# Spreading the out-projection matmuls between the score bursts, and letting turned results share the value banks

## The chip, the cores and the metric

The kernel runs on one core of a Trainium2 chip. The metric is device time in microseconds, as the median of several runs. The ratio of two kernels is the mean time of the one's fast runs over the mean time of the other's fast runs from the same rounds, so it is not quite the ratio of the medians that are quoted. All runs here are classed as fast. Yet they have two levels, which the granted TensorE clock tells apart: the kernel before takes 399.7 to 402.0 us (once 403.0) when the mean granted clock is 0.999 or more, and 402.8 to 404.6 us when it is 0.987 to 0.992. So a difference of one per cent is read below from the traces (the length of a batch), not from the medians alone.

Engine names in the profile: PE is TensorE, PEld its weight loads, DVE is VectorE, ACT is ScalarE, POOL is GpSimd.

## The reference

Causal attention with 16 extra keys per head, then a gated feed-forward block:

```python
B, H, S, Nb, D = 8, 8, 576, 16, 64
k_all = concat([beacon_k, k]); v_all = concat([beacon_v, v])
scores = q @ k_all.T / 8             # causal mask on the 576 own keys
a = softmax(scores); attn = a @ v_all
x = attn.transpose(0, 2, 1, 3).reshape(B * S, H * D)        # 4608 x 512
g = x @ w_gate; val = x @ w_val                             # 512 x 1536
out = (gelu(g) * val) @ w_out                               # 1536 x 512
```

## The kernel before

Batch `b` of the attention is interleaved with the out-projection of token chunk `b - 1`, so that TensorE has work while ScalarE makes exponentials. The heads go in pairs `m = 0..3`. A pair has four score chunks; chunks 0 and 2 ("ab") and then 1 and 3 ("cd") go through two PSUM buffers `s`. Chunk 1 has to wait until the exponential of chunk 0 has read its buffer, and chunk 3 likewise for chunk 2. After the attention of a batch, the gate and value matmuls of a chunk run in one stretch of 96 matmuls of 512 columns.

The kernel lays out PSUM as eight banks: four for `s`, two for the values `x`, one for out-projection sums `o`, and one spare bank `t` (which also takes the sum of the first of a chunk's four output rows). A finished out-projection sum is evicted, that is, VectorE copies it out of its bank.

```python
def attend(b, m, wide=False):                   # values: 30 matmuls of 65 columns
    x_ps = psum_x.tile([P, 1024], FP32, name="x_ps", tag="x")   # two banks, one tile
    # (wide: the same from psum_s)
    ...
            c0 = SLOT[j] + hi * DV              # j = 0,1,2 in the first bank, 3,4 in the second
            ... mm(x_ps[:, c0 : c0 + DV], expT[...], v_sb[...]) ...

def normalize(b, m):
    ...
    for c0, j0, n in ((0, 0, 6), (512, 6, 4)):  # first bank, second bank
        reciprocal(r, x[:, :, D:DV])
        tensor_tensor(out=y_sb[:, j0 : j0 + n, :], in0=x[:, :, 0:D], in1=r, op=mult)

def turn(b, m):                                 # transposes of the normalized result
    y_ps = psum_t.tile([P, 1024], BF16, name="y_ps", tag="t")
    for j in (4, 3, 2, 1, 0):
        transpose(y_ps[:, Q_LO[j] : Q_LO[j] + n], y_sb[0:n, j, :])
    tensor_copy(xT_sb[:, m, b * S : (b + 1) * S], y_ps[:, 0:S])
...
# batches 1 to 7; o(n) issues the next n of 48 out matmuls (12 per 128 rows of output)
o(6); ab(0); o(10); cd(0); o(8)
for m in range(1, NPAIR):
    ab(m)
    av(m - 1)                                   # attend + normalize
    cd(m)
    o(6 if m < NPAIR - 1 else 5)
    turn(b, m - 1)
av(3); o(7); turn(b, 3)
```

`keep(...)`, left out here, holds every engine to program order. The waits between engines are not written by hand: the language derives them from the tiles that an instruction reads and writes.

The softmax here doesn't subtract the row's maximum and nothing guards it: scores larger than these inputs give would overflow.

Of the kernel before, what the change touches and what calls it, by code (L numbers as in the profile page):

```python
# [7 lines left out]
P = 128  # L8
B, H, S, NB, D = 8, 8, 576, 16, 64
# [8 lines left out]
NPAIR = H // 2  # L18
# [3 lines left out]
S_LO = [0, 112, 240, 368, 496]  # L22
# [17 lines left out]

Q_LO = [0, 112, 240, 368, 448]
SLOT = [0, 2 * DV, 4 * DV, 512, 512 + 2 * DV]
QK_SCALE = 0.125

FP32 = mybir.dt.float32
BF16 = mybir.dt.bfloat16
# [7 lines left out]
def kernel(  # L54
# [12 lines left out]
    nc = tc.nc  # L67
    keep = tc.keep_in_program_order
# [9 lines left out]
    psum_t = ctx.enter_context(tc.tile_pool(name="psum_t", bufs=1, space=bass.MemoryType.PSUM))  # L78
# [3 lines left out]
    ident = const.tile([P, P], BF16, name="ident", tag="ident")  # L82
# [4 lines left out]
    xT_sb = const.tile([P, NPAIR, N_TOK], BF16, name="xT_sb", tag="xT_sb")  # L87
# [56 lines left out]
    def load_v(b):  # L144
        load_keys(v, beacon_v, v_ring[b % NRING][:, :, :, 0:D], b)
# [9 lines left out]
    def mm(out_ap, lhsT, rhs, start, stop, **kw):  # L155
        keep(nc.tensor.matmul(out_ap, lhsT, rhs, start=start, stop=stop, **kw))  # L156

    def act(out_ap, in_ap, func, **kw):
        keep(nc.scalar.activation(out_ap, in_ap, func, **kw))  # L159
# [27 lines left out]
    def warm(b, m, n):  # L187
        w_ps = psum_o.tile([P, D_MODEL], FP32, name="w_ps", tag="o")
        for _ in range(n):
            mm(w_ps, ident, qkT[:, m, 1, 0:512], True, True)  # L190
# [14 lines left out]
    def scores(b, m, c):  # L205
        i = b * NPAIR + m
        if c == 0:
            exp_of[i] = epool.tile([P, 2, EXP_W], BF16, name="expT", tag="expT")
        expT = exp_of[i]
        s_ps = psum_s.tile([P, 2, 512], FP32, name="s_ps", tag="s")  # L210
        for t, s_lo, w, col in CHUNKS[c]:
            for hi in range(2):
                r = slice(64 * hi, 64 * hi + 64)
                mm(
                    s_ps[:, hi, col : col + w],
                    qkT[r, m, 1, t * P : (t + 1) * P],
                    qkT[r, m, 0, NB + s_lo : NB + s_lo + w],
                    True,
                    True,
                )  # L220
        o, w = CHUNK_OFF[c], CHUNK_W[c]
        act(expT[:, :, o : o + w], s_ps[:, :, 0:w], ACT.Exp, scale=QK_SCALE)
        if b:
            masks(b, m, c)
# [29 lines left out]
    def attend(b, m, wide=False):  # L254
        i = b * NPAIR + m
        if wide:
            x_ps = psum_s.tile([P, 1024], FP32, name="xs_ps", tag="s")
        else:
            x_ps = psum_x.tile([P, 1024], FP32, name="x_ps", tag="x")
        expT, v_sb = exp_of.pop(i), v_ring[b % NRING]  # L260
        x_of[i] = x_ps
        for j in range(5):
            for hi in range(2):
                c0 = SLOT[j] + hi * DV
                for t in range(j + 1):
                    e0 = EXP_OFF[t] + Q_LO[j] - S_LO[t]
                    mm(
                        x_ps[:, c0 : c0 + DV],
                        expT[0 : KROWS[t], hi, e0 : e0 + P],
                        v_sb[0 : KROWS[t], t, 2 * m + hi, 0:DV],  # L270
                        t == 0,
                        t == j,
                        skip_group_check=True,
                    )

    y_of = {}

    def normalize(b, m):
        i = b * NPAIR + m
        x_ps = x_of.pop(i)  # L280
        r_sb = npool.tile([P, 10, 1], FP32, name="r_sb", tag="r_sb")
        y_sb = npool.tile([P, 10, D], BF16, name="y_sb", tag="y_sb")
        y_of[i] = y_sb
        for c0, j0, n in ((0, 0, 6), (512, 6, 4)):
            x = x_ps[:, c0 : c0 + n * DV].rearrange("p (j d) -> p j d", d=DV)
            r = r_sb[:, j0 : j0 + n, :]
            keep(nc.vector.reciprocal(r, x[:, :, D:DV]))  # L287
            keep(
                nc.vector.tensor_tensor(  # L289
                    out=y_sb[:, j0 : j0 + n, :], in0=x[:, :, 0:D], in1=r.to_broadcast([P, n, D]), op=ALU.mult  # L290
                )
            )

    def turn(b, m):
        y_sb = y_of.pop(b * NPAIR + m).rearrange("p (j e) d -> p j (e d)", e=2)
        y_ps = psum_t.tile([P, 1024], BF16, name="y_ps", tag="t")
        for j in (4, 3, 2, 1, 0):
            n = P if j else S_LO[1]
            keep(nc.tensor.transpose(y_ps[:, Q_LO[j] : Q_LO[j] + n], y_sb[0:n, j, :], ident[0:n, 0:n]))  # L299
        keep(nc.vector.tensor_copy(xT_sb[:, m, b * S : (b + 1) * S], y_ps[:, 0:S]))  # L300


    h_of, o_of = {}, {}
# [26 lines left out]
    def out_mms(ci, u0, u1, wide=lambda ti: False):  # L330
        for u in range(u0, u1):
            ti, fi = divmod(u, F_TILES)
            if u == 0:
                o_of[ci] = [opool.tile([P, 4, D_MODEL], FP32, name="o_sb", tag="o_sb"), None]
            if fi == 0:
                if wide(ti):
                    o_of[ci][1] = psum_t.tile([P, D_MODEL], FP32, name="o_ps", tag="t")
                else:
                    o_of[ci][1] = psum_o.tile([P, D_MODEL], FP32, name="o_ps", tag="o")
            o_sb, o_ps = o_of[ci]  # L340
            mm(
                o_ps,
                h_of[ci][:, fi, ti * P : (ti + 1) * P],
                wo_sb[:, fi, :],
                fi == 0,
                fi == F_TILES - 1,
            )
            if fi == F_TILES - 1:
                keep(nc.vector.tensor_copy(o_sb[:, ti, :], o_ps))  # L349
                n0 = ci * CH + ti * P  # L350
                keep(nc.sync.dma_start(out=out[n0 : n0 + P, :], in_=o_sb[:, ti, :]))
# [23 lines left out]
    for b in range(B):  # L375
        u = [0]

        def o(n):
            if b:
                out_mms(b - 1, u[0], u[0] + n, lambda ti: ti == 0)  # L380
                u[0] += n

        def ab(m):
            for c in AB:
                scores(b, m, c)

        def cd(m):
            for c in CD:
                scores(b, m, c)

        def av(m, wide=False):
            attend(b, m, wide)
            normalize(b, m)

        keep(nc.scalar.preload_act_table_set(SET_EXP))
        if b == 0:
            for m in range(NPAIR):
                ab(m)
                if m == NPAIR - 1:
                    for mm_ in (0, 1, 2):  # L400
                        for c in AB + CD:
                            if mm_ == 2 or (mm_ == 1 and c in CD):
                                masks(0, mm_, c)
                    av(0)
                    for c in AB:
                        masks(0, m, c)
                else:
                    transpose_pe(0, m + 1, psum_x, "x")
                    if m == 2:
                        for mm_, cs in ((0, AB + CD), (1, AB)):  # L410
                            for c in cs:
                                masks(0, mm_, c)
                cd(m)
                if 1 <= m < NPAIR - 1:
                    warm(b, m, 5)
            for c in CD:
                masks(0, NPAIR - 1, c)
            av(1)
            av(2, wide=True)
            turn(b, 0)  # L420
            turn(b, 1)
            av(3)
            turn(b, 2)
            turn(b, 3)
        else:
            o(6)
            ab(0)
            o(10)
            cd(0)
            o(8)  # L430
            for m in range(1, NPAIR):
                ab(m)
                av(m - 1)
                cd(m)
                o(6 if m < NPAIR - 1 else 5)
                turn(b, m - 1)
            av(3)
            o(7)
            turn(b, 3)
        keep(nc.scalar.preload_act_table_set(SET_GELU))  # L440
        for fi in range(F_TILES):
            gate_val(b, fi, kk_late=fi == 0)
            if b == 0 and 6 <= fi < 10:
                transpose_pe(1, fi - 6, psum_x, "x")
            if fi == 0:
                if b + 2 < B:
                    load_qk(b + 2)
                    load_v(b + 2)
                if NPERM <= b + 1 < B:
                    transpose_dma(b + 1)  # L450
# [34 lines left out]
```

## Time and profile before

| | before |
|---|---|
| time, median of 4 runs | 400.13 us |
| span of the profiled run | 398.9 us |
| length of a batch (one gate/value start to the next, batches 2 to 7) | 42.45 us |
| of it gate/value, 96 matmuls at 0.216 us | 20.7 us |
| PE waits for exponentials (list of waits) | 11.3 us, 25 times |

The engine shares and the clock row of the page (forty slices of the span, tenths of full clock, 9 is 90% or more):

```profile
PE 368.8 (92%) x2960; PEld 186.1 (47%) x3010; DVE 168.1 (42%) x345; ACT 186.2 (47%) x252; POOL 155.5 (39%) x277
...
PEclk9999999999999999999999999999999999999999
```

PE is the limit, and it has its full clock. The list of PE's waits (engine, line, whom it waited for: us in total, times, longest) shows what the change aims at:

```profile
PE s_ps L156 <- ACT expT L159: 11.3, 25, 0.9
...
PE y_ps L299 <- DVE xT_sb L300: 3.4, 2, 1.9
```

One pair of batch 4 on PE's timeline (start, duration, engine, line, operation, output <- inputs, count; in brackets the idle time before and who ended it):

```profile
190.23 0.59 PE L156 MATMUL s_ps<-qkT 64*128 64x512 bf16 x4
190.75 1.09 PE L156 MATMUL x_ps<-v_sb,expT 128*128 128x65 bf16 x30
191.79 0.38 PE L156 MATMUL s_ps<-qkT 64*128 64x64 bf16 x6
192.63 0.27 PE L156 MATMUL s_ps<-qkT 64*128 64x208 bf16 x2 [0.45 <-ACT expT L159]
192.83 1.47 PE L156 MATMUL o_ps<-wo_sb,hT_sb 128*128 128x512 bf16 x5
194.13 0.44 PE L299 MATMUL y_ps<-ident,y_sb 128*128 128x128 bf16 x5
```

The last score chunk of a pair waits 0.45 us for its buffer, three times in each of seven batches: 9.5 us. The five transposes of a turn stand together; from their start at 194.13 to the next pair at 194.50 they take 0.37 us. Some matmul records are missing from this trace (2960 of 3010), so a group's count can be one short.

VectorE's side of the same pair: the first reciprocal starts at 191.87, although the twelve matmuls of the bank that it reads are the first twelve of the thirty that began at 190.75. The last product, which the first transpose needs, ends at 192.79 + 0.42 = 193.21, which is 1.42 us after PE has gone on from the values to the next scores (191.79).

```profile
191.87 0.20 DVE L287 RECIPROCAL r_sb<-x_ps 128x6 f32<-128x6 f32 x1 [0.85 <-PE x_ps L156]
192.10 0.56 DVE L289 TENSOR_TENSOR y_sb<-x_ps,r_sb 128x384 bf16<-128x384 f32 x1
192.58 0.17 DVE L287 RECIPROCAL r_sb<-x_ps 128x4 f32<-128x4 f32 x1
192.79 0.42 DVE L289 TENSOR_TENSOR y_sb<-x_ps,r_sb 128x256 bf16<-128x256 f32 x1
```

### The profile page before, as it was taken

The page shows a single profiled execution, that of the slowest core. Times are in us where ns is not written, and L with a number is a line of the kernel's source. Part 1 is how long each engine was busy: PE and PEld are TensorE (multiplying, and loading weights), DVE is VectorE, ACT ScalarE, POOL GpSimd, SP SyncE. Part 2 cuts the span into 40 slices and gives each one's busy share as a digit, 9 for nine tenths or more (in the row PEclk, how much of TensorE's full clock was granted, in tenths as well). Part 3 has the DMA queues.
Part 4 walks back from the last instruction along what each step waited for, and adds up shares of the span by engine and source line. Part 5 has one row for each costly group of instructions (what it writes and reads, how often), then busy time and mean ns, then how long its engine had stood idle before and what let it go on. Part 6 is the DMA issues. An engine that isn't in the chain of part 4 may idle for free.

```text
span 398.9 us, 7336 instructions
## 1 busy us (share of the span) xinstructions
PE 368.8 (92%) x2960; PEld 186.1 (47%) x3010; DVE 168.1 (42%) x345; ACT 186.2 (47%) x252; POOL 155.5 (39%) x277
## 2 busy tenths in 40 slices
PE   3878999999989998999899999999899989999996
PEld 1454444544454445544554445444544455444442
DVE  1384653533354425433444335343444254333332
ACT  2752247533772377336653575337723673332210
POOL 8722394781358324940487047903300141000000
PEclk9999999999999999999999999999999999999999
DMA  7999997499109961997089913992042010000012
GB/s 89 180 206 204 175 131 93 51 141 159 58 28 148 137 75 49 116 156 87 30 99 139 117 54 49 161 142 60 30 92 54 30 54 26 2 0 28 26 53 105
DMA packets 139153, 36.23 MB, mean 91 GB/s; under 512 B 126832, under 2 KB 134512, under 8 KB 139120
## 3 DMA queue, kind: packets, MB, share of 16 engines
q0 software_dynamic: 103984, 19.14, 63.7%
q1 hardware_dynamic: 35136, 16.62, 20.3%
q8 instruction: 23, 0.38, 0.4%
q14 instruction: 10, 0.08, 0.1%
HBM read 38.27 MB, written 9.44 MB: 120 GB/s over the span
## 4 chain that ended last, share of the span: by engine, by line
PE 81%; ACT 10%; DVE 4%; issue 2%; DMA 1%; POOL 0%; ACTq 0%; POOLq 0%; DVEq 0%
PE gv_ps L156 46%; PE o_ps L156 24%; ACT expT L159 10%; PE s_ps L156 6%; PE y_ps L299 2%; PE x_ps L156 2%; PE t_ps L168 1%; DVE y_sb L289 1%; DVE qkT L179 1%; DMA kb<-in_beacon_k_dram 1%; DVE expT L236 1%; PE w_ps L156 0%; DVE hT_sb L325 0%; ACT ge_sb L159 0%; POOL qk L110 0%
## 5 line engine op out<-in xcount | busy, mean ns | idle before, releaser
L159 ACT ACTIVATE ge_sb<-gv_ps 128x512 bf16<-128x512 f32 x108 | 64.5, 597 | 160.6 <-PE gv_ps L156 160.6
L325 DVE TENSOR_TENSOR hT_sb<-gv_ps,ge_sb 128x512 bf16<-128x512 f32 x108 | 74.7, 692 | 123.4 <-ACT ge_sb L159 123.4
L159 ACT ACTIVATE expT<-s_ps 128x1024 bf16<-128x1024 f32 (+3 forms) x128 | 101.2, 867 | 36.7 <-PE s_ps L156 36.6
L156 PE MATMUL gv_ps<-xT_sb,wv_sb 128*128 128x512 bf16 x430 | 111.9, 379 | 0.1
L156 PE MATMUL gv_ps<-xT_sb,wg_sb 128*128 128x512 bf16 x414 | 109.9, 379 | 1.0
L239 POOL TENSOR_SCALAR_AFFINE_SELECT expT<-expT 128x256 bf16<-128x256 bf16 (+2 forms) x140 | 51.5, 387 | 142.9 <-ACT expT L159 142.9
L156 PE MATMUL o_ps<-wo_sb,hT_sb 128*128 128x512 bf16 x403 | 100.5, 380 | 2.2 <-issue 1.1
L156 PEld LDWEIGHTS <-wv_sb 128*128 128x128 bf16 x432 | 42.2, 98 | 51.0
L156 PEld LDWEIGHTS <-wg_sb 128*128 128x128 bf16 x432 | 41.5, 98 | 48.3
L156 PEld LDWEIGHTS <-hT_sb 128*128 128x128 bf16 x432 | 38.9, 98 | 45.7 <-issue 1.7
L156 PE MATMUL s_ps<-qkT 64*128 64x336 bf16 (+5 forms) x384 | 39.4, 290 | 13.0 <-ACT expT L159 11.3
L349 DVE COPY o_sb<-o_ps 128x512 f32<-128x512 f32 x36 | 24.9, 691 | 46.3 <-PE o_ps L156 43.9
L110 POOL DMA_DIRECT2D v_sb<-in_v_dram x40 | 33.8, 862 | 14.0 <-DMA wv_sb<-in_moe_w_val_dram 3.6
L156 PEld LDWEIGHTS <-expT 128*128 128x128 bf16 (+1 forms) x960 | 31.1, 97 | 9.6 <-POOL expT L239 8.5
L156 PE MATMUL x_ps<-v_sb,expT 128*128 128x65 bf16 x930 | 33.6, 193 | 0.6 <-DVE y_sb L289 0.6
L289 DVE TENSOR_TENSOR y_sb<-x_ps,r_sb 128x384 bf16<-128x384 f32 (+1 forms) x62 | 30.4, 491 | 2.1
L156 PEld LDWEIGHTS <-qkT 64*128 64x128 bf16 x384 | 15.1, 95 | 30.8 <-issue 22.3
L110 POOL DMA_DIRECT2D q_sb<-in_q_dram x30 | 25.3, 855 | 6.1 <-DMA wo_sb<-in_moe_w_out_dram 6.1
L110 POOL DMA_DIRECT2D k_sb<-in_k_dram x30 | 25.4, 891 | 0.0
L300 DVE COPY xT_sb<-y_ps 128x576 bf16<-128x576 bf16 x32 | 14.5, 453 | 19.0 <-PE y_ps L299 19.0
L287 DVE RECIPROCAL r_sb<-x_ps 128x6 f32<-128x6 f32 (+1 forms) x62 | 11.4, 184 | 22.7 <-PE x_ps L156 22.7
L299 PE MATMUL y_ps<-ident,y_sb 128*128 128x128 bf16 (+1 forms) x160 | 14.1, 218 | 3.4 <-DVE xT_sb L300 3.4
(33 smaller groups left out, 91.2 us busy)
## 6 DMA issues: line engine op xcount, KB each, us to landing
out_dram<-o_sb SPq DMA_DIRECT2D x36, 256.0 KB, 2.0
v_sb<-in_v_dram POOLq DMA_DIRECT2D x24, 128.0 KB, 9.6
q_sb<-in_q_dram POOLq DMA_DIRECT2D x24, 128.0 KB, 4.7
k_sb<-in_k_dram POOLq DMA_DIRECT2D x18, 128.0 KB, 7.5
wg_sb<-in_moe_w_gate_dram POOLq DMA_DIRECT2D x3, 512.0 KB, 11.5
wv_sb<-in_moe_w_val_dram POOLq DMA_DIRECT2D x3, 512.0 KB, 13.3
wo_sb<-in_moe_w_out_dram POOLq DMA_DIRECT2D x1, 1536.0 KB, 23.4
v_sb<-in_v_dram POOLq DMA_DIRECT2D x8, 112.0 KB, 8.1
```

Source lines behind the costliest of these rows:

```text
L110: keep(nc.gpsimd.dma_start(out=out_ap, in_=in_ap))
L156: keep(nc.tensor.matmul(out_ap, lhsT, rhs, start=start, stop=stop, **kw))
L159: keep(nc.scalar.activation(out_ap, in_ap, func, **kw))
L168: keep(nc.tensor.transpose(out_ap, in_ap, ident[0:n, 0:n]))
L179: nc.vector.tensor_copy(qkT[:, m, :, NB:SK].rearrange("p w (t r) -> p w t r", r=6), t_ps[:, 0:2, 0:S].rearrange("p w (r t) -> p w t r", r=6),)
L239: nc.gpsimd.affine_select(out=d, in_=d, pattern=[[0, 2], [1, n]], compare_op=ALU.is_ge, fill=0.0, base=NB if t == 0 else 0, channel_multip ...
L287: keep(nc.vector.reciprocal(r, x[:, :, D:DV]))
L289: nc.vector.tensor_tensor(out=y_sb[:, j0 : j0 + n, :], in0=x[:, :, 0:D], in1=r.to_broadcast([P, n, D]), op=ALU.mult)
L299: keep(nc.tensor.transpose(y_ps[:, Q_LO[j] : Q_LO[j] + n], y_sb[0:n, j, :], ident[0:n, 0:n]))
L300: keep(nc.vector.tensor_copy(xT_sb[:, m, b * S : (b + 1) * S], y_ps[:, 0:S]))
L325: nc.vector.tensor_tensor(out=h_of[ci][:, fi, :], in0=gv_ps[:, 1, :], in1=ge_sb, op=ALU.mult)
L349: keep(nc.vector.tensor_copy(o_sb[:, ti, :], o_ps))
```

## The change

The intent: put out matmuls in front of the "cd" scores, so that the exponentials have freed the buffers when these scores come. Out matmuls then cross the boundary between two output rows inside a group, so their sums get a second bank (`t`). The turned results, which used `t`, move into the unused columns of the value banks: a part in the first bank, a part in the second, each copied out on its own.

```diff
+Y_HI, Y_LO = 800, 1600
...
-        y_of[i] = y_sb
+        y_of[i] = (y_sb, x_ps.bitcast(BF16))
...
     def turn(b, m):
-        y_ps = psum_t.tile([P, 1024], BF16, name="y_ps", tag="t")
-        for j in (4, 3, 2, 1, 0):
-            transpose(y_ps[:, Q_LO[j] : Q_LO[j] + n], y_sb[0:n, j, :])
-        tensor_copy(xT_sb[:, m, b * S : (b + 1) * S], y_ps[:, 0:S])
+        y_sb, y_ps = y_of.pop(b * NPAIR + m)
+        for js, base, q0, q1 in (((4, 3), Y_HI, S_LO[3], S), ((2, 1, 0), Y_LO, 0, S_LO[3])):
+            for j in js:
+                transpose(y_ps[:, c0 : c0 + n], y_sb[0:n, j, :])
+            tensor_copy(xT_sb[:, m, b * S + q0 : b * S + q1], y_ps[:, base : base + q1 - q0])
...
-                out_mms(b - 1, u[0], u[0] + n, lambda ti: ti == 0)
+                out_mms(b - 1, u[0], u[0] + n, lambda ti: ti % 2 == 0)
...   # batch 0
-            av(1); av(2, wide=True); turn(b, 0); turn(b, 1); av(3); turn(b, 2); turn(b, 3)
+            av(1, wide=True); turn(b, 0); av(2); turn(b, 1); av(3, wide=True); turn(b, 2); turn(b, 3)
...   # batches 1 to 7
-            o(6); ab(0); o(10); cd(0); o(8)
+            o(6); ab(0); o(7); cd(0); o(6)
             for m in range(1, NPAIR):
                 ab(m)
                 av(m - 1)
+                o(3)
                 cd(m)
-                o(6 if m < NPAIR - 1 else 5)
                 turn(b, m - 1)
+                o(4 if m < NPAIR - 1 else 6)
-            av(3); o(7); turn(b, 3)
+            av(3); o(6); turn(b, 3)
```

(The diff is shortened to one statement per call; statements that stood on lines of their own are joined.)

More of the change, by code (lines that the diff above doesn't have):

```diff
@@ L294, in turn @@
     def turn(b, m):
-        y_sb = y_of.pop(b * NPAIR + m).rearrange("p (j e) d -> p j (e d)", e=2)
-        y_ps = psum_t.tile([P, 1024], BF16, name="y_ps", tag="t")
-        for j in (4, 3, 2, 1, 0):
-            n = P if j else S_LO[1]
-            keep(nc.tensor.transpose(y_ps[:, Q_LO[j] : Q_LO[j] + n], y_sb[0:n, j, :], ident[0:n, 0:n]))
-        keep(nc.vector.tensor_copy(xT_sb[:, m, b * S : (b + 1) * S], y_ps[:, 0:S]))
+        y_sb, y_ps = y_of.pop(b * NPAIR + m)
+        y_sb = y_sb.rearrange("p (j e) d -> p j (e d)", e=2)
+        for js, base, q0, q1 in (((4, 3), Y_HI, S_LO[3], S), ((2, 1, 0), Y_LO, 0, S_LO[3])):
+            for j in js:
+                n = P if j else S_LO[1]
+                c0 = base + Q_LO[j] - q0
+                keep(nc.tensor.transpose(y_ps[:, c0 : c0 + n], y_sb[0:n, j, :], ident[0:n, 0:n]))
+            keep(
+                nc.vector.tensor_copy(
+                    xT_sb[:, m, b * S + q0 : b * S + q1], y_ps[:, base : base + q1 - q0]
+                )
+            )
     h_of, o_of = {}, {}
@@ L417 @@
                 masks(0, NPAIR - 1, c)
-            av(1)
-            av(2, wide=True)
+            av(1, wide=True)
             turn(b, 0)
+            av(2)
             turn(b, 1)
-            av(3)
+            av(3, wide=True)
             turn(b, 2)
@@ L427 @@
             ab(0)
-            o(10)
+            o(7)
             cd(0)
-            o(8)
+            o(6)
             for m in range(1, NPAIR):
@@ L433 @@
                 av(m - 1)
+                o(3)
                 cd(m)
-                o(6 if m < NPAIR - 1 else 5)
                 turn(b, m - 1)
+                o(4 if m < NPAIR - 1 else 6)
             av(3)
-            o(7)
+            o(6)
             turn(b, 3)
```

## The prediction

> **What bounds it.** PE is 92% busy (engine shares) and holds 81% of the chain of waits; TensorE clock 1.0. A batch repeats every 42.45 us (chain: gate/value starts at 120.87, 163.32, 205.77). Gate/value is gapless: 96 matmuls at 0.216 us (timeline). The Trainium skill, "TensorE: Matmul & The Clock Gate", section "Wait — 56ns, not 53.3ns?", has 215.7 ns for N=512; this trace agrees. The change touches the other 21.8 us, whose PE work is 48 out matmuls (10.4 us), scores, values, transposes.
>
> **What waits there.** List of waits: PE for the exponentials, 11.3 us in 25 waits. On the timeline, each of 3 pairs per batch shows 0.45 us before the last score chunk: it needs the exponential that only starts 1.42 us after the pair's first scores. 21 x 0.45 = 9.5 us is what the change can win, 2.4%.
>
> **What changes, m=1..3, costed from the timeline** (time from the pair's first scores): scores 0.52, values 1.05, now out x3 0.65, then the last two score chunks from 2.22 to 2.62; the buffer is free at 2.36 and needed about 2.42, so the 0.45 us wait goes. But the turn now follows at 2.62, and its first transpose needs the whole normalization, which ends 1.42 us after the last value matmul (191.80 to 193.22): 3.0. About 0.43 us wait returns there; before, six out matmuls covered it. Then transposes 0.37, out x4 0.86: 4.28 us, against 4.27, but with 7 out matmuls instead of 6 or 5. Saved about 0.5 us a batch after the prelude; the prelude (6/7/6) gains a wait of about 0.2. Net estimate: -2.3 us over seven batches. Out evictions already did not block.
>
> **What it adds.** The turn becomes two groups in the two banks of the value tile, with a copy between: copies of 208 and 368 columns, about 0.26 and 0.34 us (between 0.156 at 16 and 0.453 at 576), +0.15 us of VectorE per turn, off the path. The danger is the order transposes 4,3 / copy / transposes 2,1,0 on one tile. In this trace a reader of half a two-bank PSUM tile waits for the tile's last matmul: the GELU, reading bank 0, starts after the eighth matmul, not the fourth; the first reciprocal starts after all 30 value matmuls, not after 12. If dependencies go by tile, transposes 2,1,0 wait for the first copy: landing 0.23 + copy 0.26 + two handoffs of 0.03 = about 0.5 us of PE idle per turn. In turns 2 and 3 an out eviction (0.69 us) sits before that copy on VectorE, so 0.9 and up to 1.5. About 2.5 us a batch, 17 us over seven. If by bank, nothing.
>
> Batch 0: values of pair 2 now wait for turn 0's copies: +0.5 to +1.5 us.
>
> **Sum.** By tile (I give it 65%): 400.5 - 2.3 + 17 + 1 = about 416. By bank: about 399. I put 413, range 397 to 420; faster 0.06, same 0.34, slower 0.60.
>
> **What would show it.** Waits: PE scores for exponentials falls from 11.3 to under 3 us; a new wait of PE transposes for normalization (y_sb), about 0.4 us x 21; PE transposes for the copy to xT_sb, 28 waits of 0.5 us or more (by tile) or almost none (by bank). Period 42.1 (by bank) or about 44.6 us. Gate/value stretches unchanged.
>
> **What would make it wrong.** Dependencies by bank or by region; PE records hiding a shorter normalization; the out matmuls waiting for evictions at the new boundaries; score buffers freed later than I read.

## The result

The changed kernel takes 422.32 us (median of 4; 421.7 to 423.3) against 400.13 us: ratio 1.0555, 95% interval 1.0525 to 1.0585. It is slower, as forecast, but 2.3 us beyond the top of the range. Its output is correct.

```profile
PE 380.8 (90%) x3010; PEld 184.6 (44%) x3010; DVE 172.1 (41%) x377; ACT 188.3 (45%) x252; POOL 155.5 (37%) x277
...
PEclk9975999999999999999999999999999999999999
```

New is a dent in the clock, in the third and fourth slices (21 to 42 us, the end of batch 0). The list of PE's waits:

```profile
PE x_ps L302 <- DVE xT_sb L304: 14.9, 30, 1.5
PE x_ps L302 <- DVE y_sb L290: 7.8, 21, 0.4
...
PE s_ps L157 <- ACT expT L160: 1.9, 4, 0.9
PE xs_ps L302 <- DVE xT_sb L304: 1.8, 2, 1.4
```

The waits for exponentials are gone but for 1.9 us. In their place stand 7.8 us of transposes (line 302) waiting for the normalization, and 16.7 us of transposes waiting for a copy out of the same tile. The pair that answers to the one shown above:

```profile
202.46 0.58 PE L157 MATMUL s_ps<-qkT 64*128 64x512 bf16 x4
202.97 1.09 PE L157 MATMUL x_ps<-v_sb,expT 128*128 128x65 bf16 x30
203.90 0.81 PE L157 MATMUL o_ps<-wo_sb,hT_sb 128*128 128x512 bf16 x3
204.64 0.48 PE L157 MATMUL s_ps<-qkT 64*128 64x64 bf16 x8
205.49 0.28 PE L302 MATMUL x_ps<-ident,y_sb 128*128 128x128 bf16 x2 [0.37 <-DVE y_sb L290]
206.13 0.32 PE L302 MATMUL x_ps<-ident,y_sb 128*128 128x128 bf16 x3 [0.36 <-DVE xT_sb L304]
206.30 1.03 PE L157 MATMUL o_ps<-wo_sb,hT_sb 128*128 128x512 bf16 x4
```

The eight score matmuls now run in one piece, as intended. The turn is torn in two: its second group starts 0.64 us after its first, where five transposes in a row took 0.37 us in all. VectorE's row shows the dependency: the copy of the first group starts at 205.81 and ends at 206.08, and the second group of transposes starts at 206.13.

```profile
205.81 0.27 DVE L304 COPY xT_sb<-x_ps 128x208 bf16<-128x208 bf16 x1 [0.38 <-PE x_ps L302]
```

Where the 22.0 us of span (398.9 to 420.9) lie, from the starts of the gate/value stretches:

| stretch | before | after | more |
|---|---|---|---|
| start to first gate/value matmul (batch 0's attention) | 32.27 | 35.89 | 3.62 |
| batch 0's gate/value and batch 1's attention | 46.15 | 50.86 | 4.71 |
| each of the next six batches | 42.45 | 44.68 | 2.23 |
| last gate/value start to the end | 65.8 | 66.0 | 0.2 |

Six times 2.23 is 13.4 us, and one more such amount sits in the second row. The other 2.5 us of that row and the 3.6 us of the first are batch 0's: 6.1 us. A view of stretches of time with each engine's busy time and, after POOL, the granted clock shows why. First the changed kernel, then the kernel before:

```profile
27.00:32.00 5.00, 3.18 (x52) 3.02 (x52) 2.14 (x7) 0.00 (x0) 1.72 (x2) 0.50 1.25 205
...
36.00:41.00 5.00, 5.00 (x16) 1.76 (x14) 1.04 (x2) 0.60 (x1) 2.49 (x3) 0.55 1.28 206
```

```profile
27.00:32.00 5.00, 1.87 (x45) 1.80 (x46) 3.52 (x10) 0.00 (x0) 1.53 (x2) 1.00 1.25 205
36.00:41.00 5.00, 5.00 (x25) 2.27 (x24) 2.08 (x3) 1.61 (x4) 2.21 (x3) 1.00 1.28 206
```

From about 27 us to about 41 us the clock of the changed kernel is halved (the trace's clock record has one stretch of 13.65 us at 0.5, apart from the last 1.4 us of the span). In the same five microseconds from 36 to 41, PE gets 16 matmuls through in place of 25. The Trainium skill, "TensorE: Matmul & The Clock Gate", section "What's actually happening", tells of two states, full and half clock, ruled by how busy PE was in windows of about 3.4 us. The trace agrees with the two states and with the windows: 13.65 us are four windows of 3413 ns, the length that the page gives. How busy PE must be in a window, no run here shows.

PE's waits in this stretch, in the changed kernel and then in the kernel before:

```profile
26.67 0.32 PE L302 MATMUL x_ps<-ident,y_sb 128*128 128x128 bf16 x3 [1.49 <-DVE xT_sb L304]
27.43 1.81 PE L157 MATMUL x_ps<-v_sb,expT 128*128 128x65 bf16 x30 [0.44 <-DVE xT_sb L304]
30.84 0.47 PE L302 MATMUL xs_ps<-ident,y_sb 128*128 128x128 bf16 x3 [1.39 <-DVE xT_sb L304]
34.55 0.46 PE L302 MATMUL x_ps<-ident,y_sb 128*128 128x128 bf16 x3 [1.39 <-DVE xT_sb L304]
```

```profile
28.60 0.45 PE L299 MATMUL y_ps<-ident,y_sb 128*128 128x128 bf16 x5 [1.92 <-DVE xT_sb L300]
31.77 0.44 PE L299 MATMUL y_ps<-ident,y_sb 128*128 128x128 bf16 x5 [1.53 <-DVE xT_sb L300]
```

The changed kernel has more waits here, but none as long as the longest of the kernel before.

### The profile page after: what moved, and what is told of

It is laid out like the page before. It is cut to its first block, busy times and chain, and to the rows that moved or that the text cites. A ratio compares the mean times of both kernels' runs of the same rounds, so it can differ in the third digit from the quotient of the medians.

```text
span 420.9 us, 7417 instructions
## 1 busy us (share of the span) xinstructions
PE 380.8 (90%) x3010; PEld 184.6 (44%) x3010; DVE 172.1 (41%) x377; ACT 188.3 (45%) x252; POOL 155.5 (37%) x277
## 4 chain that ended last, share of the span: by engine, by line
PE 72%; DVE 15%; ACT 7%; DMA 2%; issue 2%; POOL 1%; POOLq 0%
PE gv_ps L157 44%; PE o_ps L157 12%; DVE y_sb L290 7%; PE x_ps L157 7%; ACT expT L160 4%; PE s_ps L157 3%; PE x_ps L302 3%; DVE r_sb L288 2%; DVE o_sb L356 2%; DMA qk<-in_k_dram 2%; DVE xT_sb L304 2%; ACT L402 2%; ACT ge_sb L160 1%; PE w_ps L157 1%; POOL qk L111 1%
## 5 line engine op out<-in xcount | busy, mean ns | idle before, releaser
L160 ACT ACTIVATE expT<-s_ps 128x1024 bf16<-128x1024 f32 (+3 forms) x128 | 103.2, 861 | 38.8 <-PE s_ps L157 34.0
L157 PE MATMUL gv_ps<-xT_sb,wg_sb 128*128 128x512 bf16 x432 | 113.8, 383 | 0.0
L157 PE MATMUL gv_ps<-xT_sb,wv_sb 128*128 128x512 bf16 x432 | 113.1, 381 | 0.0
L157 PE MATMUL o_ps<-wo_sb,hT_sb 128*128 128x512 bf16 x432 | 106.8, 379 | 0.0
L157 PE MATMUL s_ps<-qkT 64*128 64x336 bf16 (+5 forms) x384 | 37.0, 291 | 4.2 <-ACT expT L160 1.9
L111 POOL DMA_DIRECT2D v_sb<-in_v_dram x40 | 34.0, 870 | 16.7 <-DMA wv_sb<-in_moe_w_val_dram 3.7
L302 PE MATMUL x_ps<-ident,y_sb 128*128 128x128 bf16 (+1 forms) x150 | 18.5, 221 | 23.7 <-DVE xT_sb L304 14.9
L157 PEld LDWEIGHTS <-expT 128*128 128x128 bf16 (+1 forms) x960 | 33.1, 100 | 11.8 <-issue 6.8
L290 DVE TENSOR_TENSOR y_sb<-x_ps,r_sb 128x384 bf16<-128x384 f32 (+1 forms) x60 | 29.5, 491 | 2.1
L157 PEld LDWEIGHTS <-qkT 64*128 64x128 bf16 x384 | 13.8, 95 | 32.7 <-issue 27.3
L302 PEld LDWEIGHTS <-y_sb 128*128 128x128 bf16 (+1 forms) x160 | 10.8, 100 | 36.5 <-issue 20.7
```

The lines of the kernel that those rows point to most:

```text
L111: keep(nc.gpsimd.dma_start(out=out_ap, in_=in_ap))
L157: keep(nc.tensor.matmul(out_ap, lhsT, rhs, start=start, stop=stop, **kw))
L160: keep(nc.scalar.activation(out_ap, in_ap, func, **kw))
L290: nc.vector.tensor_tensor(out=y_sb[:, j0 : j0 + n, :], in0=x[:, :, 0:D], in1=r.to_broadcast([P, n, D]), op=ALU.mult)
L302: keep(nc.tensor.transpose(y_ps[:, c0 : c0 + n], y_sb[0:n, j, :], ident[0:n, 0:n]))
```

## The experiments

Theory: the loss in the seven later batches is the copy that stands between the two groups of transposes; the waits follow the declared tile, so writing the second bank waits for a copy that reads only the first. The loss in batch 0 is the same wait plus a halved clock. Rivals: the new places of the out matmuls; slow or conflicting accesses to the value banks; a clock that drops for other reasons. Eleven kernels ran, and all gave correct outputs. "Batch" is the usual (median) spacing of the gate/value starts in batches 2 to 7.

| run | time us | ratio to before | batch us |
|---|---|---|---|
| before | 400.1 | 1 | 42.45 |
| changed | 422.3 | 1.0555 | 44.68 |
| a1 batch 0 as before | 416.2 | 1.0380 | 44.68 |
| a2 only batch 0 changed | 406.0 | 1.0121 | 42.45 |
| a3 copies after all transposes | 399.5 | 0.9968 | 42.33 |
| a4 fillers in batch 0 | 420.6 | 1.0484 | 44.68 |
| b1 new places only | 408.1 | 1.0156 | 43.57 |
| b2 shared banks only | 425.6 | 1.0608 | 45.99 |
| b3 turn in the idle out bank | 393.3 | 0.9786 | 41.41 |
| b4 two one-bank value tiles | 388.4 | 0.9664 | 40.82 |
| c1 a3 with the turn later | 399.6 | 0.9935 | 42.34 |
| c2 b4 retimed | 389.1 | 0.9679 | 41.01 |
| c3 a2 with fillers | 403.3 | 1.0048 | 42.45 |

### a1 and a2: batch 0 apart from the rest

a1 is the changed kernel in which batch 0 keeps its old order and a turn through the spare bank; a2 is the kernel before with the new batch 0.

```diff
 # a1, batch 0
-            av(1, wide=True); turn(b, 0); av(2); turn(b, 1); av(3, wide=True); turn(b, 2); turn(b, 3)
+            av(1); av(2, wide=True); turn_t(b, 0); turn_t(b, 1); av(3); turn_t(b, 2); turn_t(b, 3)
```

> The changed kernel with batch 0 alone put back as before (turns into the spare bank, one copy, old order). Theory (batch 0 cost 3.6 us in its own tail and 2.5 us in its gate/value stage through the halved TensorE clock): 416.2 us, mean clock 1.0, seven later batches still 44.68 us each. Rival (the clock drop and the loss come from the seven batches): about 420 to 422 us, clock still 0.98.

> The kernel before with batch 0 alone as in the change. Theory: 406.3 us, a half-clock stretch of some 10 to 14 us between 27 and 41 us, later batches 42.45 us. Rival (batch 0 costs only what its longer VectorE chain explains, 1 us): 401 to 402 us, clock 1.0.

a1 took 416.18 us, a2 406.04 us. a1's profiled run has clock 1.0; a2's has the same 13.7 us at half clock, and its first gate/value stretch is lengthened like the changed kernel's. So batch 0 costs 422.3 - 416.2 = 6.1 us in the changed kernel, and nearly as much alone (406.0 - 400.4 = 5.6 us in a2's own rounds), so it costs this independently of the other batches. The rivals' numbers (420 to 422, and 401 to 402) are excluded.

### a3: the copies after all transposes

```diff
-        for js, base, q0, q1 in parts:          # transposes of a part, then its copy
-            for j in js: transpose(...)
-            tensor_copy(...)
+        for js, base, q0, q1 in parts:
+            for j in js: transpose(...)
+        for js, base, q0, q1 in parts:
+            tensor_copy(...)
```

> The changed kernel with all five transposes of a turn first and both copies after them; same banks, same places. Theory (the transposes 2,1,0 wait for the first copy only because it stands before them in the program and both touch one tile): the waits of transposes for the copy, 14.9 us, vanish; the waits for the normalization, 7.8 us, stay; 406 to 409 us. Rival (writing into the value banks is itself slow, or the turn waits for the normalization anyway and the two waits overlap): 418 to 422 us.

It took 399.54 us, against 422.3: moving two statements takes away the whole loss, more than was expected (406 to 409 us). A batch falls from 44.68 to 42.33 us, 2.35 us for four turns, 0.59 us per turn. That is more than the 0.43 us of idle per turn that the list of waits shows for batches 1 to 7 (12.0 us over 28 turns in a1), because PE's record counts as busy time in which PE could already have gone on: the first two transposes have a record of 0.28 us in the pair shown, but where nothing holds up the next ones they start 0.12 us after the first (b4, below). Batch 0 recovers as well: its first gate/value matmul starts at 31.58 us, and the clock of the profiled run is 0.998. In PE's waits the copy is gone from the transposes and the normalization stays:

```profile
PE x_ps L303 <- DVE y_sb L290: 8.0, 22, 0.4
...
PE s_ps L157 <- ACT expT L160: 1.9, 4, 0.9
```

### a4 and c3: the clock in batch 0

Both put 13 extra matmuls into the gaps of batch 0's end, a4 into the changed kernel, c3 into a2.

```diff
             turn(b, 0)
+            warm(b, 3, 3)
             av(2)
+            warm(b, 3, 6)
             turn(b, 1)
             av(3, wide=True)
+            warm(b, 3, 4)
```

> The changed kernel with 13 idle-filling matmuls put into the gaps of batch 0's tail, nothing else. Theory (PE idles so long in batch 0's tail that its clock is halved for some 13 us, which stretches two value bursts and the first 12 gate/value matmuls): clock 1.0, about 418.5 us although more work is issued. Rival (the halved clock has another cause, or the fillers cost what they win): clock 0.98 or time 422 us and more.

> a2 (batch 0 alone as in the change) with the 13 fillers of a4. Theory (the halved clock costs 2.5 us and more in batch 0, and the fillers keep it whole): clock 1.0 and 402.5 to 404 us against 406.0 of a2. Rival (the clock drop is not worth its look, as a4's time fell by only 1.7 us): 405 to 407 us with clock 1.0.

a4 came out between its two expectations. Its profiled run has the full clock, and the span falls by 3.6 us (420.9 to 417.3), but the median time only by 1.7 us, to 420.6. In a4's runs the time exceeds the span by 1.9 to 3.4 us where nearly all other runs have 1.7 to 1.8; why is open. c3 was run to settle it, and gave 403.32 us against a2's 406.04 (ratios 1.0048 and 1.0121, on different chips; their intervals, 0.9994 to 1.0101 and 1.0056 to 1.0186, overlap). The mean clock of c3's four runs is 0.992 to 0.999, that of a2's 0.983 to 0.987. The clock of c3's profiled run is 1.0 where a2's was halved; a2 first, then c3:

```profile
36.00:41.00 5.00, 4.78 (x16) 1.85 (x15) 0.69 (x1) 0.60 (x1) 2.42 (x3) 0.63 1.28 206
```

```profile
36.00:41.00 5.00, 5.00 (x25) 2.27 (x24) 2.08 (x3) 1.79 (x3) 2.49 (x3) 1.00 1.28 205
```

In a2 the first gate/value start and the stretch after it are later and longer than in the kernel before by 3.12 + 2.35 = 5.5 us; with fillers by 1.92 + 0.22 = 2.1 us. So of batch 0's loss some 3.3 us are the halved clock, and some 2.1 us are the longer waits themselves. These figures include a small shift from before the programs differ: the last scores of pair 2 came at 19.83 us in the kernel before, at 18.77 in a2 and at 19.33 in c3. Counted from there, a2 loses 6.5 us and c3 2.6 us, which makes the clock's share 3.9 us.

### b1 and b2: each part of the change alone

b1 takes the new places but keeps the turn in the spare bank with one copy (and batch 0 as before). b2 takes the shared banks but keeps the old places (batch 0 as before).

```diff
 # b1: before, with only this
-            o(6); ab(0); o(10); cd(0); o(8)
+            o(6); ab(0); o(7); cd(0); o(6)
-    ab(m); av(m - 1); cd(m); o(6 if m < NPAIR - 1 else 5); turn(b, m - 1)
+    ab(m); av(m - 1); o(3); cd(m); turn(b, m - 1); o(4 if m < NPAIR - 1 else 6)
-            av(3); o(7); turn(b, 3)
+            av(3); o(6); turn(b, 3)
 # b2: a1, with these three hunks reversed
```

> Part 1 alone: the kernel before with the new places of the out matmuls and of the turn, but turns still into the spare bank with one copy, batch 0 untouched. Theory: the 0.45 us waits for exponentials go, about 0.37 us for the normalization comes in their place (21 times), and out matmul 24, now in the middle of a group, waits about 0.9 us for the eviction of its only bank (7 times): 402 to 405 us. Rival (the places alone are the loss): 410 us or more.

> Part 2 alone: turns in the value banks in two groups with a copy between, out matmuls over two banks, but the old places; batch 0 as before. Theory (the copy between the groups is the loss, wherever the turn stands; behind an out eviction it costs about 1 us, else 0.5): 416 to 423 us with no wait for the normalization but still 9 to 10 us of waits for exponentials. Rival (the loss needs the new places): 400 to 403 us.

b1 took 408.1 us, between the two expectations. Its waits are those the theory named, but a batch is 1.1 us longer, not 0.3 to 0.7. a3 shows where this lies: it has the same places, the turn in one piece too, but two out banks, and its batch is 43.57 - 42.33 = 1.24 us shorter. In b1's batch 4 the out matmul that waits for the eviction starts 1.38 us after the start of a group of two, which take 0.43 us: 0.95 us lost. In the third pair the next output row begins right after the turn, 0.59 us after its first transpose instead of 0.29 us, when VectorE has just ended the eviction of the row before (205.09 to 205.77, out matmul at 205.83): another 0.30 us, of which the list of waits shows nothing. PE's waits in b1, then in b2:

```profile
PE y_ps L299 <- DVE y_sb L289: 7.8, 21, 0.4
PE o_ps L156 <- DVE o_sb L349: 5.5, 7, 0.8
...
PE s_ps L156 <- ACT expT L159: 1.8, 3, 0.9
```

```profile
PE x_ps L310 <- DVE xT_sb L312: 16.1, 28, 0.8
PE s_ps L157 <- ACT expT L160: 11.1, 24, 0.9
...
PE x_ps L157 <- DVE xT_sb L312: 3.1, 7, 0.4
```

b1 shows why the change wanted the second out bank (5.5 us of out matmuls waiting for an eviction), and that the places alone give the 0.45 us back: the normalization waits 0.37 us where the exponential waited 0.45 us. b2 took 425.6 us, longer than the whole change, with all the waits for the copy and all the waits for exponentials. So the main loss belongs to the shared tile with a copy in its middle, and the new places do not cause it. The 3.1 us of values waiting for the copies (once a batch) were not expected: a turn late in its pair leaves the value tile occupied when the next values come.

### c1: the turn behind the second out group

```diff
 # a3, with
-                turn(b, m - 1)
                 o(4 if m < NPAIR - 1 else 6)
+                turn(b, m - 1)
```

> a3 (both copies last) with each turn moved behind the second out group, so that the normalization is covered. Theory (sharing the value banks keeps the value tile busy until the turn's copies are done, and with the turn last the next pair's values stand 0.5 us behind it): the waits for the normalization (8 us) go, but the values now wait some 0.35 us for the copies, about 20 times: 397 to 400 us, little better than a3. Rival (the tile is free in time): 391 to 394 us.

It took 399.61 us, as expected. The wait for the normalization is gone, and this one has come:

```profile
PE x_ps L157 <- DVE xT_sb L306: 9.2, 22, 1.7
```

Sharing the value tile has a price of its own, then: the next pair's values stand behind the turn's copies. While the tile is one, the turn is either too early for the normalization (a3, 8.0 us) or too late for the next values (c1, 9.2 us).

### b3 and b4: two ways out

b3 starts from the kernel before. It gives the out sums two banks as in the change, and lets each turn use whichever of these two is not accumulating.

```diff
+            def turn_spare(m):
+                turn(b, m, "o" if (u[0] // F_TILES) % 2 == 0 else "t")
-            o(6); ab(0); o(10); cd(0); o(8)
+            o(6); ab(0); o(9); cd(0); o(5)
-    ab(m); av(m - 1); cd(m); o(6 if m < NPAIR - 1 else 5); turn(b, m - 1)
+    ab(m); av(m - 1); o(3); cd(m); o(4); turn_spare(m - 1)
```

> A version meant to win: each turn goes into whichever of the two out banks is not accumulating, one copy, behind the second out group (out groups 6/9/5, then 3 and 4 per pair, then 7); batch 0 as before. Theory (both waits of 0.45 and 0.37 us go, nothing new comes): 391 to 394 us. Rival (once these waits go the exponentials bound the pairs): 397 to 400 us.

b4 is a1 with the value tile declared as two tiles of one bank each. The banks, the columns and the order of instructions on PE in batches 1 to 7 are the change's; in batch 0, where the key and query transposes use the same banks, one copy becomes two.

```diff
-            x_ps = psum_x.tile([P, 1024], FP32, name="x_ps", tag="x")
+            x_ps = tuple(psum_x.tile([P, 512], FP32, name=f"x{s}_ps", tag=f"x{s}") for s in "ab")
...
-                        x_ps[:, c0 : c0 + DV],
+                        x_ps[bank][:, c0 : c0 + DV],
...
-        for js, base, q0, q1 in (((4, 3), Y_HI, S_LO[3], S), ((2, 1, 0), Y_LO, 0, S_LO[3])):
+        for js, y_ps, base, q0, q1 in (((4, 3), xa, Y_HI, S_LO[3], S), ((2, 1, 0), xb, Y_LO - 1024, 0, S_LO[3])):
```

> The changed kernel, batch 0 order as before, with the two-bank value tile declared as two one-bank tiles; same banks, same instruction order in the seven batches (batch 0's key and query copies split in two). Theory (waits go by declared tile, not by bank or region): the waits for the copy vanish, the first reciprocal starts after 12 of 30 value matmuls so the wait for the normalization vanishes too: 391 to 396 us, batches about 41.2 us. Rival (waits go by bank, or the chip's bank conflicts cause them): no change from a1, 416 us.

b3 took 393.31 us. b4 took 388.44 us: the ratio to before is 0.9664 (0.9603 to 0.9726), and it beats both kernels of this study. One pair of b4 on PE's timeline:

```profile
187.70 0.59 PE L157 MATMUL s_ps<-qkT 64*128 64x512 bf16 x4
188.22 0.54 PE L157 MATMUL xa_ps<-v_sb,expT 128*128 128x65 bf16 x12
188.59 0.71 PE L157 MATMUL xb_ps<-v_sb,expT 128*128 128x65 bf16 x18
189.36 0.59 PE L157 MATMUL o_ps<-wo_sb,hT_sb 128*128 128x512 bf16 x2
189.88 0.48 PE L157 MATMUL s_ps<-qkT 64*128 64x64 bf16 x8
190.30 0.29 PE L320 MATMUL xa_ps<-ident,y_sb 128*128 128x128 bf16 x2
190.42 0.33 PE L320 MATMUL xb_ps<-ident,y_sb 128*128 128x128 bf16 x3
190.59 1.03 PE L157 MATMUL o_ps<-wo_sb,hT_sb 128*128 128x512 bf16 x4
```

No wait is left in this pair. The second group of transposes starts 0.12 us after the first; with one tile it was 0.64. And the first reciprocal of this pair starts at 188.79, 0.57 us after the first value matmul, where it was 191.87 - 190.75 = 1.12 us in the kernel before, so the normalization is ready when the turn comes:

```profile
188.79 0.20 DVE L294 RECIPROCAL r_sb<-xa_ps 128x6 f32<-128x6 f32 x1 [0.73 <-PE xa_ps L157]
190.62 0.27 DVE L322 COPY xT_sb<-xa_ps 128x208 bf16<-128x208 bf16 x1 [0.49 <-PE xa_ps L320]
```

Against a1, which has the same batch 0 but for the split copy, both effects follow from the declaration alone, so both waits were made by the declared tile, and neither by the bank nor by the hardware behind it. That using one bank while VectorE reads another is safe is what the Trainium skill states in "PSUM — Partial Sum Buffer", section "PSUM bank collisions raise a hardware error": the unit to guard is the bank (or a 32-partition quadrant of it). b4 agrees: its output is correct with VectorE copying from the first bank (from 190.62) while PE still transposes into the second (until 190.75 by its record).

### c2: b4 retimed

```diff
-            o(6); ab(0); o(7); cd(0); o(6)
+            o(6); ab(0); o(9); cd(0); o(5)
-                o(4 if m < NPAIR - 1 else 6)
+                o(4)
-            av(3); o(6); turn(b, 3)
+            av(3); o(7); turn(b, 3)
```

> b4 (two one-bank value tiles) with out groups 6/9/5 before the first pair, 3 and 4 in every pair and 7 at the end, in place of 6/7/6, 3 and 4, 3 and 4, 3 and 6, 6. Theory (what is left to win is the 0.25 us wait of the first pair's last scores for their buffer): 386 to 387.5 us. Rival (nothing left): 388.4 us or more, as the values of the last pair may now wait for their masks.

It took 389.12 us with a batch of 41.01 us, so nothing was won. The rival was right: the last pair's values now wait for POOL's masks, 1.7 us in seven waits, which is about 0.25 us per batch.

## Why the prediction was right or wrong

- **Direction and main cause: right.** It named the danger, the order "transposes 4,3 / copy / transposes 2,1,0 on one tile", and read from the trace before (GELU after the eighth matmul, reciprocal after the thirtieth) that a reader of half a tile waits for the whole. b4 shows that this is so, by taking away the shared declaration alone.
- **Size of it: right.** "About 2.5 us a batch, 17 us over seven"; a3 measures 2.35 us a batch, 16.5 us. The batch was forecast at 44.6 us and is 44.68. The terms behind it were less good, and that their sum is so close is partly luck: of the 28 waits forecast at "0.5 us or more", and at 0.9 to 1.5 us where an eviction stands before the copy, those of batch 4 idle 0.36, 0.36, 0.48 and 0.52 us, so the eviction adds only about 0.1 us; each turn loses another 0.16 us that the list of waits doesn't show.
- **Waits for exponentials "under 3 us": right**, 1.9 us. **A new wait for the normalization of "about 0.4 us x 21": right**, 7.8 us in 21 waits.
- **"Net estimate: -2.3 us over seven batches": too favourable.** Without the copy's wait (a3) a batch is 42.33 us against 42.45, so 0.8 us over seven. The places alone had hardly a gain to give, since the wait for the normalization replaced that for the exponentials.
- **"Batch 0: values of pair 2 now wait for turn 0's copies: +0.5 to +1.5 us": wrong; this is the step that failed.** Batch 0 costs 6.1 us (422.3 in the changed kernel, 416.2 in a1). The wait that the term names is there, but it is 0.44 us of this. The term left out that the torn turns wait in batch 0 as well (1.4 to 1.5 us each in three of its four, since the copy stands behind a normalization on VectorE; the old turns have two waits there, 3.4 us in all), and that PE's clock was then halved for 13.65 us. By a2 and c3 the clock alone is some 3.3 to 3.9 us, and "gate/value stretches unchanged" was wrong for the first of them for that reason.
- **The stated number, 413, lay between two cases.** The by-tile case was put at "about 416"; with batch 0 at its measured size it would have been 416 + 5 = 421, against 422.3, and most of the rest is the net estimate (-0.8 us in place of -2.3). The 35% given to "by bank" pulled the number and the range down, so that the top of the range, 420, lay below the result.

Open: which share of idle time halves the clock. The kernel before has a stretch, 27 to 32 us, with PE busy for only 1.87 of 5.00 us, and kept its full clock in its profiled run; the changed kernel had PE busy for 1.50 of 3.00 us just before its clock fell, but a3 had 1.35 of 3.00 us in the same stretch (24 to 27 us) and kept it. Nor is the loss peculiar to the new batch 0: b4's profiled run, with batch 0 in its old order, is at half clock for 3.41 us from 28.0 us on, and the runs of the kernel before with a mean clock of 0.987 to 0.992 were at half clock for some 6 to 10 us if these two states are all there is (an estimate, twice the missing share of 402 us; these runs kept no trace, so where is not known). Also open is why a4's time fell by less than its span.

## What to carry to other kernels

Before an instruction that writes is put behind one that reads, ask whether both touch the same declared tile: here a copy between two groups of transposes cost 0.59 us per turn although the groups lay in different banks, and declaring one tile per bank turned a 3.8% loss (a1) into a 3.4% gain (b4). When a wait is covered by moving work, look at what that work had been covering: the six out matmuls had hidden the normalization, whose 0.37 us wait took the place of the exponentials' 0.45 us. And where a change adds idle time to a stage in which PE is already half idle, look at the clock too: here its loss outlasted the stage, to 40.5 us, 4.6 us into the gate/value matmuls.

## What the Trainium skill lacked or had wrong

- "TensorE: Matmul & The Clock Gate", section "HAM oscillation — how this bites in real kernels", gives the rule in the form "no PE-idle gaps >~3.4µs". Here no wait in the end of batch 0 was longer than 1.5 us, and the clock was halved for 13.65 us all the same. The page's section "A second HAM failure mode: psum-queue depth-cycling" does tell of frequent short idles, but no section has a share of busy time below which the clock falls; nor do these runs give one (the kernel before was busy for 1.87 of 5.00 us and kept its clock, with one wait of 1.92 us).
- "PSUM — Partial Sum Buffer", section "PSUM bank collisions raise a hardware error", tells to guard by bank. No page says that waits derived from declared tiles can be coarser than that: with one two-bank tile the second group of transposes came 0.64 us after the first, with two one-bank tiles 0.12 us (b4).
